# Attention and channel mix on one core: how the first three token groups' q and k are turned, and another order of the opening's steps

## The chip, the cores and the metric

The program runs on one core of one Trainium2 chip. The metric is device time in microseconds, the median of several runs; lower is better. TensorE (PE in the rows, its weight loads PEld), VectorE (DVE), ScalarE (ACT) and SyncE (SP, which only issues transfers here) each work through a queue of their own, in order.

## What is computed

Chunked attention (chunks of 64 tokens, 8 heads of 64) over 8 sequences of 576 tokens, then an RWKV-like channel mix over its 512 outputs.

```python
scores = scale * np.matmul(q_c, k_c.transpose(0, 1, 2, 4, 3))     # within a chunk
attn = softmax(scores);  x = np.matmul(attn, v_c)                  # heads side by side: 512 wide
xk = mu_k * x + (1.0 - mu_k) * x_prev                              # x_prev: the token before
xr = mu_r * x + (1.0 - mu_r) * x_prev
k = np.maximum(xk @ w_k, 0.0)                                      # 512 -> 1024
v = k * k @ w_v                                                    # 1024 -> 512
r = 1.0 / (1.0 + np.exp(-(xr @ w_r)))
return (r * v).astype(np.float32)
```

The weights arrive as 64-bit floats, so their transfers carry 8 bytes for a number, and the kernel makes two float parts (high and low) of each.

## The kernel before

The 4608 tokens are worked in 18 groups of 256 (two tiles of 128). A large product is done as three products of high and low parts (PASSES, line 577). Groups 2 to 17 are written by `group` in the order of the table GROUP. The opening, which covers the loading and conversion of all weights, the attention of tiles 0 to 5 and most of groups 0 and 1, is written in the order of the table START: each word is one step, and each step goes to the end of its engine's queue. No scheduler moves anything after that.

A word is task, number and, after a colon, the engine that does it (A for ScalarE, D for VectorE). The tasks that matter here:

- `nk0`, `nq0`: transfers of group 0's k and q in natural layout, 512 KB each; `v0`: of tile 0's v in four pieces; `swk0` to `swk3`, `swr0`, `swr1`, `swv0` to `swv3`: of pieces of the three weights, 1 MB each. All go through SP's queue.
- `cwk0.0` to `.2` and `hwk0.0`, `.1`: the conversion of such a piece on ScalarE and VectorE.
- `T0.0` to `T0.7`: the turning of group 0's q (0 to 3) and k (4 to 7). Even numbers are eight small products with the identity on TensorE (function `f_tr`, line 357; tiles trq and trk), odd ones copy the result to qT or kT (`f_move`). The partition of a natural tile is a token pair, so a step before takes the even or the odd tokens of the whole group: 128 partitions in, 64 columns of the array, 128 columns streamed, and both column halves of the array at work.
- `S0.0` to `.5`: scores of tile 0 (line 400, 16 products of 64x64 in the four quarters of the array), maximum, subtraction, exponential, sum, division. Scores of a tile need its tokens of qT and kT, which here means all four turning steps of the group.
- `P0.0`, `.1`, `.2`: turning of the probabilities (line 464, pt), copy, product with v (line 484, xps); `Mk`, `Mr`: the token mixes; `K00` to `K03`: the first product of group 0 by quarters of w_k (line 593, pk); `R00`, `R01`: the gate's product by tiles (line 647, pr); `V`: the product with w_v (line 681, pv).
- `W:n`: n products of a 128x128 zero tile with itself (line 1186, warm), whose result nobody reads. They occupy TensorE's queue like any other product. Each shows as two records in the trace, as every plain float product does.

```python
            if name == "W":
                for _ in range(int(e)):
                    nc.tensor.matmul(warm, idle, idle, start=True, stop=True)
            else:
                fn, engine_of = first.pop(name)
                fn(e or engine_of)
```

The rotating PSUM tiles set further waits: ps_k has two buffers for trq, trk and pk together, ps_s has one for scores and turned probabilities.

Of the kernel before, what the change touches and what calls it, by code (L numbers as in the profile page):

```python
# [16 lines left out]
P = 128  # L17
# [7 lines left out]


START = """
mu.0:A nk0.0 nq0.0 swr0.0 W:9 T0.4 T0.6 T0.5:A swr1.0 T0.7:A T0.2 T0.3:D nk1.0 T0.0 mu.1 T0.1:A
cwr0.1:A W:1 S0.0 cwr0.0:A P0.3:D S0.1:D S0.2:D S0.3:A cwr0.2:D v0.0 S0.4:D W:7 S1.0 nq1.0 W:5
T1.6 S1.1:D cwr1.1:A mu.2:A S0.5:D S1.2:D T1.4 P0.0 hwr0.0:A swk3.0 cwr1.0:A T1.7:A S1.3:A  # L30
cwr1.2:D P0.1:A W:3 P0.2 T1.5:A hwr0.1:D S1.4:D P0.4:A hwr1.0:A Mk0.0:D S1.5:D T1.0 T1.2 T1.1:A
Mr0.0:D v1.0 swk0.0 P1.0 Mk0.1:D T1.3:A P1.3:D P1.1:A Mr0.1:A nk2.0 cwk3.0:A W:3 S2.0 Mr0.2:D
S2.1:D nq2.0 W:5 S3.0 P1.2 P1.4:A hwr1.1:D v2.0 S2.2:D R00.0 S2.3:A cwk0.0:A T2.4 cwk3.1:A
S3.1:D Mk1.0:D S2.4:D Mr1.0:D cwk0.1:A S2.5:D T2.5:A T2.6 S3.2:D swk2.0 swk1.0 Mk0.2:A Mr1.1:A
P2.0 T2.7:A T2.2 Mk1.1:D cwk0.2:D T2.0 Mk0.3:D P2.1:A Mk1.2:A S3.3:A Mr1.2:D T2.3:A P2.2
cwk3.2:D hwk0.0:A hwk0.1:D Mk1.3:D T2.1:A S3.4:D P2.3:D hwk3.0:A cwk2.0:A cwk2.1:A S3.5:D
hwk3.1:D P2.4:A v3.0 R01.0 cwk2.2:D cwk1.1:A P3.3:D cwk1.0:A K00.0 K00.1:A P3.0 cwk1.2:D
hwk2.0:A K03.0 P3.1:A S4.0 hwk1.0:A Mk2.0:D hwk2.1:D P3.2 K03.1:A swv1.0 K00.2:A P3.4:A v5.0
Mr2.0:D K03.2:A hwk1.1:D Mr2.1:D S5.0 Mk2.1:D K02.0 R00.1:A Mk3.0:D Mr2.2:D cwv1.0:A swv0.0
Mr3.0:D swv2.0 K00.3:A Mk3.1:D K01.0 K00.4:D R01.1:A cwv1.1:A Mk2.2:A K03.3:D Mr3.1:A Mr3.2:D  # L40
v4.0 K01.1:A Mk3.2:A K03.4:D K01.2:D Mk2.3:D Mk3.3:D cwv2.0:A cwv2.1:A K02.1:A R10.0 cwv2.2:D
cwv0.0:A R11.0 K10.0 S4.1:D cwv1.2:D K02.2:A K11.0 cwv0.1:A hwv2.0:A K01.3:A cwv0.2:D K01.4:D
hwv0.0:A P4.3:D bq3.0 K10.1:A K10.2:A hwv2.1:D K12.0 hwv1.0:A swv3.0 R10.1:A hwv0.1:D S4.2:D
R11.1:A S5.1:D V001.0 S4.3:A hwv1.1:D S5.2:D V001.1 V001.2 V001.3 S4.4:D K02.3:A K10.3:A S4.5:D
S5.3:A K02.4:D cwv3.0:A S5.4:D P4.0 V001.4 cwv3.1:A S5.5:D K12.1:D P4.1:A cwv3.2:D P5.0
hwv3.0:D P5.1:A V001.5 P4.2 hwv3.1:D K12.2:D P5.2 K12.3:A P4.4:A K10.4:D bk3.0 K11.1:D Mk4.0:D
V001.6 K11.2:A V001.7 K11.3:A K13.0 D7.0:D V001.9:D K11.4:D P5.3:D V001.8:D K12.4:D V11.0 V11.1
V10.0 v6.0 Mr4.0:D K13.1:A V10.1 K13.2:A V10.2 P5.4:A K13.3:D V10.3 V11.2 V10.4 Mk4.1:D Mk5.0:D
K13.4:D V10.5 V11.3 V11.4 V11.5 Mk4.2:D V11.6 Mk5.1:D Mr4.1:A Mr4.2:D V10.6 v7.0 D7.1:D V11.7
D6.0:D Mk4.3:D D6.1:D Mk5.2:D Mr5.0:D V11.8:D Mk5.3:D Mr5.1:D V10.7 V10.8:D Mr5.2:D  # L50
"""


# [26 lines left out]
def tile_chunk_attention_channel_mix(  # L80
# [501 lines left out]
    def moe_k(g, fp):  # L582
        def f_mm(_):
            pk = T[f"pk{g}{fp}"] = ps_k.tile([P, 2, G], F32, tag="k", name=f"pk_{g}_{fp}")
            xk = T[f"xk{g}"]
            for e in range(2):
                f = 2 * fp + e
                n = 0
                for cb in range(NB):
                    for a, b in PASSES:  # L590
                        parts = tok if (g > SPLIT and f == n == 0) or (g, f, n) == (1, 0, 0) else (slice(0, G),)
                        for part in parts:
                            nc.tensor.matmul(  # L593
                                pk[:, e, part],
                                wk[a][:, cb, f * P : (f + 1) * P],
                                xk[b][:, cb, part],
                                start=(n == 0 and part is parts[0]),
                                stop=(n == 3 * NB - 1),
                                skip_group_check=True,
                            )  # L600
                        n += 1

        def f_relu(e):
            if g >= SPLIT:
                if fp == 0:
                    T[f"rr{g}"] = mx.tile([P, NF, G], F32, tag="kk", name=f"rr_{g}", bufs=4)
                r = T[f"rr{g}"][:, 2 * fp : 2 * fp + 2, :]
            else:
                r = mo.tile([P, 2, G], F32, tag="relu", name=f"relu_{g}_{fp}")
            T[f"r{g}{fp}"] = r  # L610
            if e == "D":
                nc.vector.tensor_scalar(r, T[f"pk{g}{fp}"], 0.0, None, ALU.max)
            else:
                nc.scalar.activation(r, T[f"pk{g}{fp}"], AF.Relu)  # L614

        def f_sq(e):
            r = T[f"r{g}{fp}"]
            if e == "D":
                nc.vector.tensor_tensor(r, r, r, ALU.mult)
            else:  # L620
                nc.scalar.activation(r, r, AF.Square)  # L621

        def f_hi(e):
            if f"kk{g}" not in T:
# [664 lines left out]
```

## Time and profile before

| | |
|---|---|
| median of 3 runs | 562.23 us (562.0 to 562.52) |
| the profiled execution's own time | 561.84 us |
| its span, first to last instruction | 560.1 us |
| busy share of the span: PE / PEld / DVE / ACT | 99% / 94% / 83% / 62% |
| granted TensorE clock | 1.00 |

The time of the profiled execution is 1.74 us over its span, and 0.39 us under the median of the runs. The busy share of PE includes the fillers `W`, so it doesn't say how much of the span is useful.

### The profile page before, as it was taken

The numbers are of one execution on the slowest core, as the hardware profiler recorded it, in microseconds if no ns is written. First come the engines' busy times: TensorE is split into PE (matmuls) and PEld (weight loads), VectorE is DVE, ScalarE is ACT, GpSimd is POOL, SyncE is SP. The second block draws the span as 40 slices with busy tenths as digits, with TensorE's granted clock in tenths as the row PEclk, the third lists the DMA queues.
The fourth block names the chain that finished last, engine by engine and source line by source line (L and its number), as shares of the span: only waits on it lengthen the run. The fifth ranks groups of instructions, "written<-read, shape, count | busy, mean of one in ns | idle before, by whom it ended". The sixth has DMA issues, their size and how long they took to land.

```text
span 560.1 us, 15245 instructions
## 1 busy us (share of the span) xinstructions
PE 553.5 (99%) x6432; PEld 526.1 (94%) x6432; DVE 462.8 (83%) x789; ACT 346.1 (62%) x509; POOL 0.7 (0%) x6
## 2 busy tenths in 40 slices
PE   9999999999999999999999999999999999999997
PEld 8888999999999999999999999999999999999997
DVE  2999999999897879787888978887888788876834
ACT  5899941739474756657565747483929292938461
POOL 0000000000000000000000000000000000000000
PEclk9999999999999999999999999999999999999999
DMA  9997534444343433421243434343343402010011
GB/s 284 278 285 204 133 76 94 69 69 110 67 107 66 94 69 79 69 72 40 57 67 94 66 89 66 91 71 90 65 99 59 103 1 76 3 45 33 3 38 37
DMA packets 184276, 49.24 MB, mean 88 GB/s; under 512 B 169608, under 2 KB 176272, under 8 KB 184208
## 3 DMA queue, kind: packets, MB, share of 16 engines
q1 hardware_dynamic: 183904, 48.01, 37.9%
q8 instruction: 50, 0.82, 0.7%
q10 hardware_dynamic: 304, 0.27, 0.1%
q14 instruction: 18, 0.15, 0.1%
HBM read 38.80 MB, written 9.44 MB: 86 GB/s over the span
## 4 chain that ended last, share of the span: by engine, by line
PE 90%; ACT 7%; DMA 2%; DVE 0%; issue 0%; ACTq 0%
PE pk L593 33%; PE pr L647 16%; PE vx L870 15%; PE vyz L870 11%; PE pv L681 6%; PE xps L1058 3%; PE s L973 3%; PE pt L1040 2%; DMA k_ring<-in_k 2%; PE warm L1186 1%; ACT wk L141 1%; PE trk L357 1%; ACT wv_st L295 1%; ACT wv_st L299 1%; ACT relu L614 0%; ACT wk_st L299 0%
## 5 line engine op out<-in xcount | busy, mean ns | idle before, releaser
L593 PE MATMUL pk<-xkhi,wk 128*128 128x256 f32 (+1 forms) x1167 | 202.0, 276 | 0.2 <-ACT relu L614 0.2
L593 PEld LDWEIGHTS pk<-xkhi,wk 128*128 128x128 f32 x1167 | 177.1, 188 | 0.7 <-ACT relu L614 0.4
L593 PE MATMUL pk<-xklo,wk 128*128 128x256 f32 x576 | 160.0, 278 | 0.1
L593 PEld LDWEIGHTS pk<-xklo,wk 128*128 128x128 f32 x576 | 108.2, 188 | 0.5 <-DVE xklo L566 0.5
L614 ACT ACTIVATE rr<-pk 128x512 f32<-128x512 f32 x60 | 35.3, 589 | 114.3 <-PE pk L593 114.3
L647 PE MATMUL pr<-wr,xrhi 128*128 128x512 f32 x288 | 90.4, 395 | 0.0
L870 PE MATMUL vx<-b,ks 128*128 128x256 f32 x540 | 68.5, 276 | 0.0
L870 PE MATMUL vyz<-b,kk 128*128 128x256 f32 x540 | 68.5, 276 | 0.0
L870 PEld LDWEIGHTS vyz<-b,kk 128*128 128x128 f32 x540 | 64.5, 188 | 0.0
L870 PEld LDWEIGHTS vx<-b,ks 128*128 128x128 f32 x540 | 64.5, 188 | 0.0
L647 PEld LDWEIGHTS pr<-wr,xrhi 128*128 128x128 f32 x288 | 52.7, 188 | 10.3
L647 PE MATMUL pr<-wr,xrlo 128*128 128x512 f32 x144 | 56.2, 390 | 0.0
L899 ACT ACTIVATE u<-vx 128x256 f32<-128x256 f32 x30 | 11.5, 384 | 54.3 <-PE vx L870 54.3
L708 DVE TENSOR_TENSOR kk<-rr,kk 128x1024 fp32r<-128x1024 f32 x30 | 35.4, 1222 | 10.7 <-ACT kk L854 10.6
L621 ACT ACTIVATE rr<-rr 128x512 f32<-128x512 f32 x60 | 38.0, 633 | 1.9
L708 DVE TENSOR_TENSOR xklo<-mk,xkhi 128x1024 fp32r<-128x1024 f32 x15 | 18.4, 1225 | 25.1 <-ACT xkhi L1130 25.1
L681 PE MATMUL pv<-b,kk 128*128 128x256 f32 (+1 forms) x290 | 34.3, 278 | 0.0
L681 PEld LDWEIGHTS pv<-b,kk 128*128 128x128 f32 x290 | 33.4, 188 | 0.1
L647 PEld LDWEIGHTS pr<-wr,xrlo 128*128 128x128 f32 x144 | 27.0, 188 | 5.7
L708 DVE TENSOR_TENSOR ks<-ss,ks 128x512 fp32r<-128x512 f32 x45 | 28.3, 684 | 0.0
L1120 DVE SCALAR_TENSOR_TENSOR mk<-d,mu,x 128x256 f32<-128x256 f32 (+3 forms) x80 | 27.7, 413 | 0.4
L1120 DVE SCALAR_TENSOR_TENSOR mr<-d,mu,x 128x256 f32<-128x256 f32 (+3 forms) x80 | 27.5, 411 | 0.0
(119 smaller groups left out, 839.4 us busy)
## 6 DMA issues: line engine op xcount, KB each, us to landing
v<-in_v SPq DMA_DIRECT2D x144, 64.0 KB, 2.6
out<-sg SPq DMA_DIRECT2D x34, 256.0 KB, 2.3
q_ring<-in_q SPq DMA_DIRECT2D x192, 36.0 KB, 2.1
k_ring<-in_k SPq DMA_DIRECT2D x192, 36.0 KB, 2.2
wk_st<-in_moe_w_k SPq DMA_DIRECT2D x4, 1024.0 KB, 9.4
wv_st<-in_moe_w_v SPq DMA_DIRECT2D x4, 1024.0 KB, 7.5
wr_st<-in_moe_w_r SPq DMA_DIRECT2D x2, 1024.0 KB, 8.1
k_ring<-in_k SPq DMA_DIRECT2D x2, 512.0 KB, 7.3
```

What stands on the lines that cost most here:

```text
L593: nc.tensor.matmul(pk[:, e, part], wk[a][:, cb, f * P : (f + 1) * P], xk[b][:, cb, part], start=(n == 0 and part is parts[0]), stop=(n == ...
L614: nc.scalar.activation(r, T[f"pk{g}{fp}"], AF.Relu)
L621: nc.scalar.activation(r, r, AF.Square)
L647: nc.tensor.matmul(pr, xr[a][:, cb, tl * TT : (tl + 1) * TT], wr[b][:, cb, :], start=(n == 0), stop=(n == 3 * NB - 1),)
L681: nc.tensor.matmul(T[f"pv{g}{tl}"][:, cols[c]][:, part], kk[a][:, f, tok[tl]], quarter(f // HF, c)[:, b, f % HF, part], start=(f == 0 and ...
L708: nc.vector.tensor_tensor(to, x, y, ALU.subtract)
L870: nc.tensor.matmul(to, a[i][:, f, :], weight(w, j, f), start=first and f == 0 and n == 0, stop=f == HF - 1 and n == 2, skip_group_check=True,)
L899: nc.scalar.activation(T[f"u{g}"][n // 2][:, n % 2], src(), AF.Copy)
L973: nc.tensor.matmul(T[f"s{g}"][halves[e], j, tl, hp, :], qT[halves[j], hp, cols], kT[halves[j], hp, cols], start=True, stop=True,)
L1040: nc.tensor.transpose(out=T[f"pt{g}"][:, tl, hp, :], in_=T[f"pg{g}"][:, tl, 2 * hp : 2 * hp + 2, :], identity=ident,)
L1058: nc.tensor.matmul(T[f"xps{g}"][halves[c], 2 * j + a, tl * TT + e * CH : tl * TT + (e + 1) * CH], T[f"v{2 * g + tl}"][halves[j], hp, e, :] ...
L1120: nc.vector.scalar_tensor_tensor(out=to[:, cb, s : s + w], in0=T[f"d{g}"][:, cb, s : s + w], scalar=mu[:, cb : cb + 1], in1=T[f"xg{g}"][:, ...
```

## The change

Three things change. First, a turning step takes one tile of 128 tokens (64 token pairs, so 64 partitions) instead of every second token of the group: 16 products of 64x64 instead of 8 with 128 partitions and 128 streamed columns. Its number says which tile: `T0.0` and `T0.4` are tile 0, `T0.2` and `T0.6` tile 1. Scores of a tile then need two turning steps, not four. Second, START is another order: the two key pieces wk0 and wk1 are loaded and converted ahead of those of w_r, K00 and K01 stand ahead of R00 and R01, and the fillers stand elsewhere and number 54 instead of 33. Some copies change between ScalarE and VectorE (23 steps; ScalarE has 5 more and VectorE 5 fewer than before). Third, which first product is issued in two halves: K12's and K11's instead of K10's in group 1 (f is 2 and 4), and of the V products the first of `V001` alone.

```diff
 START = """
-mu.0:A nk0.0 nq0.0 swr0.0 W:9 T0.4 T0.6 T0.5:A swr1.0 T0.7:A T0.2 T0.3:D nk1.0 T0.0 mu.1 T0.1:A
+mu.0:A nk0.0 W:9 T0.6 T0.4 P0.3:D nq0.0 T0.7:D swk0.0 swk1.0 T0.5:A W:3 T0.0 T0.2 T0.1:A W:1
+S0.0 T0.3:A cwk0.0:A S1.0 S0.1:D v0.0 S0.2:D S1.1:D S1.2:D cwk0.1:A S0.3:A S0.4:D cwk0.2:D
...
         for nm, to in (("q", qT), ("k", kT)):
-            for r in range(2):
+            for tl in range(2):
...
                     for hp in range(HP):
-                        for j in range(2):
-                            nc.tensor.matmul(
-                                x[halves[j], hp, :],
-                                T[f"{nm}{g}"][:, j * HP + hp, r, :],
-                                ident,
-                                start=True,
-                                stop=True,
-                            )
-
-                def f_move(e, nm=nm, to=to, r=r):
-                    copy(e, to.rearrange("p h (c r) -> p h r c", r=2)[:, :, r, :], T[f"tr{nm}{r}{g}"])
+                        for r in range(2):
+                            for j in range(2):
+                                nc.tensor.matmul(
+                                    x[halves[j], hp, r, :],
+                                    T[f"{nm}{g}"][halves[tl], j * HP + hp, r, :],
+                                    ident[halves[tl], halves[tl]],
+                                    start=True,
+                                    stop=True,
+                                )
+
+                def f_move(e, nm=nm, to=to, tl=tl):
+                    to = to.rearrange("p h (t c r) -> p h t r c", t=2, r=2)
+                    copy(e, to[:, :, tl], T[f"tr{nm}{tl}{g}"])
...
-                        parts = tok if (g > SPLIT and f == n == 0) or (g, f, n) == (1, 0, 0) else (slice(0, G),)
+                        parts = tok if (g > SPLIT and f == n == 0) or (g == 1 and f in (2, 4) and n == 0) else (slice(0, G),)
...
-                            parts = tok if first and (g, tl) in ((0, 0), (1, 1)) else (slice(0, HD),)
+                            parts = tok if first and g == 0 else (slice(0, HD),)
```

TensorE's queue from the program's first product, before (trk is the turned k, trq the turned q, s scores, pt turned probabilities, xps their product with v):

```order
L1186 MATMUL warm<-idle 128x128 x9
L357 MATMUL trk_0_141<-ident,k_ring 64x128 x8
L357 MATMUL trk_0_150<-ident,k_ring 64x128 x8
L357 MATMUL trq_0_163<-ident,q_ring 64x128 x8
L357 MATMUL trq_0_174<-ident,q_ring 64x128 x8
L241 MATMUL mu_t<-ident,mus 128x8
L1186 MATMUL warm<-idle 128x128
L400 MATMUL s_188<-kT,qT 64x64 x16
L1186 MATMUL warm<-idle 128x128 x7
L400 MATMUL s_188<-kT,qT 64x64 x16
L1186 MATMUL warm<-idle 128x128 x5
L357 MATMUL trk_1_252<-ident,k_ring 64x128 x8
```

The same place after the change (lines are 4 or 5 further on):

```order
L1191 MATMUL warm<-idle 128x128 x9
L361 MATMUL trk_0_138<-ident,k_ring 64x64 x16
L361 MATMUL trk_0_155<-ident,k_ring 64x64 x16
L1191 MATMUL warm<-idle 128x128 x3
L361 MATMUL trq_0_184<-ident,q_ring 64x64 x16
L361 MATMUL trq_0_201<-ident,q_ring 64x64 x16
L1191 MATMUL warm<-idle 128x128
L405 MATMUL s_220<-kT,qT 64x64 x32
L1191 MATMUL warm<-idle 128x128 x25
L469 MATMUL pt_299<-ident,p_262 128x128 x4
L242 MATMUL mu_t<-ident,mus 128x8
L1191 MATMUL warm<-idle 128x128 x2
```

Both tiles' scores now stand together, a run of 25 fillers follows them, and group 1's turning, which stood between the scores and the first pt, has moved behind it.

TensorE's queue further on, before, from group 1's turned k to the first gate product (pr, the start of R00):

```order
L357 MATMUL trk_1_266<-ident,k_ring 64x128 x8
L464 MATMUL pt_275<-ident,p_210 128x128 x4
L1186 MATMUL warm<-idle 128x128 x3
L484 MATMUL xps_292<-pT_287,v_214 64x64 x16
L357 MATMUL trq_1_320<-ident,q_ring 64x128 x8
L357 MATMUL trq_1_329<-ident,q_ring 64x128 x8
L464 MATMUL pt_275<-ident,p_210 128x128 x4
L1186 MATMUL warm<-idle 128x128 x3
L400 MATMUL s_372<-kT,qT 64x64 x16
L1186 MATMUL warm<-idle 128x128 x5
L400 MATMUL s_372<-kT,qT 64x64 x16
L484 MATMUL xps_292<-pT_287,v_344 64x64 x16
```

After the change, from the second pt to the first key product (pk, the start of K00):

```order
L469 MATMUL pt_299<-ident,p_262 128x128 x4
L361 MATMUL trk_1_397<-ident,k_ring 64x64 x16
L489 MATMUL xps_323<-pT_314,v_316 64x64 x16
L1191 MATMUL warm<-idle 128x128 x2
L361 MATMUL trq_1_437<-ident,q_ring 64x64 x16
L1191 MATMUL warm<-idle 128x128 x4
L361 MATMUL trq_1_466<-ident,q_ring 64x64 x16
L405 MATMUL s_486<-kT,qT 64x64 x16
L1191 MATMUL warm<-idle 128x128
L361 MATMUL trk_2_512<-ident,k_ring 64x64 x16
L405 MATMUL s_486<-kT,qT 64x64 x16
L361 MATMUL trk_2_552<-ident,k_ring 64x64 x16
```

What stands ahead of the first large product is no longer R00 after two turnings but K00 after two turnings and half of group 2's. Between the rows shown, after the change, lie the first xps, a turned k and a run of 7 fillers.

SP's queue from its first transfer to group 2's k, before:

```order
L184 DMA k_ring<-in_k 128x8x128
L184 DMA q_ring<-in_q 128x8x128
L291 DMA wr_st<-in_moe_w_r 128x2x1024 x2
L184 DMA k_ring<-in_k 128x8x128
L199 DMA v_214<-in_v 64x4x64 x4
L184 DMA q_ring<-in_q 128x8x128
L291 DMA wk_st<-in_moe_w_k 128x4x512
L199 DMA v_344<-in_v 64x4x64 x4
L291 DMA wk_st<-in_moe_w_k 128x4x512
L184 DMA k_ring<-in_k 32x8x128
L184 DMA k_ring<-in_k 96x8x128
```

And after the change:

```order
L185 DMA k_ring<-in_k 128x8x128
L185 DMA q_ring<-in_q 128x8x128
L292 DMA wk_st<-in_moe_w_k 128x4x512 x2
L200 DMA v_257<-in_v 64x4x64 x4
L185 DMA k_ring<-in_k 128x8x128
L292 DMA wr_st<-in_moe_w_r 128x2x1024
L200 DMA v_316<-in_v 64x4x64 x4
L185 DMA q_ring<-in_q 128x8x128
L185 DMA k_ring<-in_k 32x8x128
L185 DMA k_ring<-in_k 96x8x128
L292 DMA wr_st<-in_moe_w_r 128x2x1024
```

Ahead of group 2's k stand three weight pieces of 1 MB where there were four; ahead of group 1's q stand three where there were two.

## Rows read from the trace of the kernel before

**Rows 1.** Busy time by stage: us, then PE, PEld, DVE, ACT, POOL.

```profile
5.26:28.95 23.69, 22.14 (x390) 19.27 (x390) 18.66 (x41) 18.28 (x26) 0.00 (x0) 1.00 1.12 303
...
62.28:560.10 497.82, 494.50 (x5644) 473.14 (x5644) 412.59 (x690) 293.68 (x436) 0.00 (x0) 1.00 0.32 69
```

**Rows 2.** Timeline of PE, 0 to 31 us: start, us, what, records, idle before.

```profile
1.05 4.21 PE L1186 MATMUL warm<-idle 128*128 128x128 f32 x18 [1.05 <-DVE idle L130]
...
9.34 0.49 PE L1186 MATMUL warm<-idle 128*128 128x128 f32 x2
9.98 0.69 PE L400 MATMUL s<-kT,qT 64*64 64x64 f32 x32 [0.15 <-ACT qT L141]
10.61 1.83 PE L1186 MATMUL warm<-idle 128*128 128x128 f32 x14
12.37 0.69 PE L400 MATMUL s<-kT,qT 64*64 64x64 f32 x32
12.99 1.38 PE L1186 MATMUL warm<-idle 128*128 128x128 f32 x10
14.30 1.97 PE L357 MATMUL trk<-ident,k_ring 128*64 128x128 f32 x32
16.23 0.63 PE L464 MATMUL pt<-ident,p 128*128 128x128 f32 x4
16.70 0.83 PE L1186 MATMUL warm<-idle 128*128 128x128 f32 x6
17.62 0.69 PE L484 MATMUL xps<-pT,v 64*64 64x64 f32 x32
18.24 1.97 PE L357 MATMUL trq<-ident,q_ring 128*64 128x128 f32 x32
20.71 0.66 PE L464 MATMUL pt<-ident,p 128*128 128x128 f32 x4 [0.49 <-DVE p L434]
21.20 0.83 PE L1186 MATMUL warm<-idle 128*128 128x128 f32 x6
22.05 0.69 PE L400 MATMUL s<-kT,qT 64*64 64x64 f32 x32
22.67 1.38 PE L1186 MATMUL warm<-idle 128*128 128x128 f32 x10
24.08 0.69 PE L400 MATMUL s<-kT,qT 64*64 64x64 f32 x32
...
25.17 0.73 PE L647 MATMUL pr<-wr,xrhi 128*128 128x512 f32 x2
...
28.95 1.97 PE L357 MATMUL trk<-ident,k_ring 128*64 128x128 f32 x32 [0.77 <-DMA k_ring<-in_k]
```

**Rows 3.** The same timeline of PE, 40 to 63 us: first rows of steps.

```profile
40.47 0.37 PE L593 MATMUL pk<-xkhi,wk 128*128 128x256 f32 x1
...
43.72 0.69 PE L400 MATMUL s<-kT,qT 64*64 64x64 f32 x32 [0.27 <-ACT pT L141]
...
45.27 0.38 PE L593 MATMUL pk<-xkhi,wk 128*128 128x256 f32 x1
...
50.84 0.63 PE L647 MATMUL pr<-wr,xrhi 128*128 128x512 f32 x2
...
56.30 0.33 PE L593 MATMUL pk<-xkhi,wk 128*128 128x128 f32 x2
...
62.28 0.38 PE L593 MATMUL pk<-xkhi,wk 128*128 128x256 f32 x1 [0.24 <-ACT relu L614]
```

**Rows 4.** Timeline of PE, 91 to 94 us: a whole group's scores.

```profile
92.25 1.16 PE L973 MATMUL s<-kT,qT 64*64 64x64 f32 x64
```

**Rows 5.** Timeline of DVE, 0 to 80 us: the second tile's low part of xk, group 0.

```profile
36.62 0.69 DVE L566 TENSOR_TENSOR xklo<-mixk,xkhi 128x512 fp32r<-128x512 f32 x1
```

**Rows 6.** Instructions on the tile trk: duration ns min/median/max, starts, forms.

```profile
L357 PEld LDWEIGHTS trk<-ident,k_ring x96: 132/137/232, 5.2 to 30.5; 128*64 128x64 f32 x96
```

**Rows 7.** Sum of five stretches of 10 us from 10 to 60 us.

```profile
sum 50.00, PE 48.19 PEld 43.10 DVE 47.45 ACT 46.94 POOL 0.00; mean PE 9.64 PEld 8.62 DVE 9.49 ACT 9.39 POOL 0.00
```

More of the change, by code (lines that the diff above doesn't have):

```diff
@@ L27 @@
 START = """
-mu.0:A nk0.0 nq0.0 swr0.0 W:9 T0.4 T0.6 T0.5:A swr1.0 T0.7:A T0.2 T0.3:D nk1.0 T0.0 mu.1 T0.1:A
[L29 to L50, printed above, removed]
+mu.0:A nk0.0 W:9 T0.6 T0.4 P0.3:D nq0.0 T0.7:D swk0.0 swk1.0 T0.5:A W:3 T0.0 T0.2 T0.1:A W:1
@@ new lines @@
+S0.0 T0.3:A cwk0.0:A S1.0 S0.1:D v0.0 S0.2:D S1.1:D S1.2:D cwk0.1:A S0.3:A S0.4:D cwk0.2:D
+S0.5:D W:25 P0.0 nk1.0 mu.1 cwk1.0:A cwk1.1:A cwk1.2:D S1.3:A hwk0.0:A swr1.0 P0.1:A v1.0 W:2
+P0.2 nq1.0 P0.4:A nk2.0 mu.2:A S1.4:D P1.3:A hwk0.1:D swr0.0 T1.6 Mk0.0:D cwr1.1:A S1.5:D
+hwk1.0:A Mr0.0:D W:7 P1.0 P1.1:A Mk0.1:D T1.4 Mr0.1:A hwk1.1:D T1.7:A P1.2 W:2 T1.0 P1.4:A
+Mk0.2:A Mk1.0:D T1.5:A T1.1:A W:4 T1.2 cwr1.0:A Mr0.2:D T1.3:A S2.0 Mk1.1:D S2.1:D Mk0.3:D W:1
+T2.4 Mk1.2:A S3.0 T2.5:A v2.0 T2.6 Mk1.3:D S2.2:D K00.0 cwr1.2:D T2.7:A nq2.0 S2.3:A S3.1:D
@@ new lines @@
+swk3.0 S2.4:D cwr0.0:A cwr0.1:A S3.2:D K00.1:A cwr0.2:D S2.5:D hwr1.0:A S3.3:A hwr0.0:A K01.0
+hwr1.1:D swk2.0 hwr0.1:D Mr1.0:D K01.1:A S3.4:D P2.0 P2.1:A T2.0 T2.2 P2.2 K01.2:A T2.1:A
+T2.3:A cwk3.1:A Mr1.1:A S3.5:D R00.0 cwk3.0:A Mr1.2:D P3.0 cwk2.0:A R01.0 P2.3:D cwk2.1:A
+cwk3.2:D hwk3.0:A K00.2:A P3.1:D v3.0 cwk2.2:D swv1.0 hwk3.1:D P2.4:A P3.3:D S4.0 hwk2.0:A
+R01.1:A S5.0 P3.2 swv2.0 Mk2.0:D P3.4:A v5.0 hwk2.1:D Mr2.0:D K03.0 Mk2.1:D swv0.0 K00.3:A
+Mr2.1:A bk3.0 Mk3.0:D R00.1:A K01.3:A K02.0 Mr2.2:D cwv2.1:A Mk3.1:D Mk2.2:D K00.4:D Mk3.2:A
@@ new lines @@
+Mk2.3:D Mk3.3:D K03.1:A K01.4:D v4.0 R10.0 K03.2:D cwv0.0:A K02.1:A K03.3:A Mr3.0:D R10.1:A
+Mr3.1:D K03.4:D cwv2.0:A cwv1.1:A S4.1:D cwv1.0:A Mr3.2:D K02.2:A K11.0 cwv0.1:A K10.0 cwv2.2:D
+hwv2.0:D hwv2.1:D cwv0.2:D K02.3:A K02.4:D R11.0 S5.1:D S4.2:D K11.1:A R11.1:A K10.1:A hwv0.0:A
+K12.0 S4.3:A cwv1.2:D hwv0.1:D swv3.0 K13.0 V001.0 hwv1.0:A S4.4:D hwv1.1:D S4.5:D S5.2:D
+V001.1 D6.1:D cwv3.0:A bq3.0 V001.2 cwv3.1:A V001.3 K10.2:A K10.3:A K11.2:A cwv3.2:D S5.3:A
+S5.4:D hwv3.0:A K11.3:A hwv3.1:D S5.5:D V001.4 P4.0 K11.4:D K12.1:A V001.5 P5.0 P4.3:D V001.6
@@ L51 @@
+P4.1:D K10.4:D D7.0:D P5.1:A K13.1:D V001.7 V001.8:D P4.2 K12.2:A K12.3:A P5.2 v6.0 V10.0
+P4.4:A P5.3:A V001.9:D V10.1 V10.2 K12.4:D Mk4.0:D K13.2:A Mk4.1:D V11.0 V10.3 V10.4 V11.1
+D6.0:D K13.3:A P5.4:D K13.4:D Mk4.2:A Mk5.0:D Mr4.0:D Mk4.3:D Mk5.1:D V10.5 D7.1:D V10.6
+Mk5.2:A Mr5.0:D V11.2 V10.7 Mr4.1:A V11.3 Mr4.2:D V11.4 v7.0 V11.5 V11.6 Mk5.3:D V10.8:D V11.7
+V11.8:D Mr5.1:A Mr5.2:D
 """
@@ L350, in move_qk, with f_tr @@
         for nm, to in (("q", qT), ("k", kT)):
-            for r in range(2):
-                def f_tr(_, nm=nm, r=r):
-                    x = T[f"tr{nm}{r}{g}"] = ps_k.tile([P, HP, P], F32, tag="k", name=f"tr{nm}{r}_{g}")
-                    for hp in range(HP):
-                        for j in range(2):
-                            nc.tensor.matmul(
-                                x[halves[j], hp, :],
-                                T[f"{nm}{g}"][:, j * HP + hp, r, :],
-                                ident,
-                                start=True,
-                                stop=True,
-                            )
-                def f_move(e, nm=nm, to=to, r=r):
-                    copy(e, to.rearrange("p h (c r) -> p h r c", r=2)[:, :, r, :], T[f"tr{nm}{r}{g}"])
+            for tl in range(2):
+                def f_tr(_, nm=nm, tl=tl):
+                    x = T[f"tr{nm}{tl}{g}"] = ps_k.tile(
+                        [P, HP, 2, CH], F32, tag="k", name=f"tr{nm}{tl}_{g}"
+                    )
+                    for hp in range(HP):
+                        for r in range(2):
[6 more added lines that the diff above has]
+                                    stop=True,
+                                )
+                def f_move(e, nm=nm, to=to, tl=tl):
+                    to = to.rearrange("p h (t c r) -> p h t r c", t=2, r=2)
+                    copy(e, to[:, :, tl], T[f"tr{nm}{tl}{g}"])
                 do(f_tr, "P")
```

## Prediction

> **What bounds the kernel now.** I read the busy time by stage first. From 62 us to the end TensorE is busy for 494.5 of 497.8 us, on work that the change doesn't touch, while VectorE and ScalarE have a sixth and two fifths of that stretch free [rows 1]. Whatever time TensorE loses or saves before 62 us therefore comes out at the end, unchanged; nothing later can take it up. So the question is one of a ledger: how much of TensorE's time in the opening is not useful work, now and after.
>
> I read that off the timeline of TensorE, from the start of one group of instructions to the start of the next, since the ends overlap. The first run of fillers (9 of them, from 1.05 us for 4.21 us) waits for the first k and is the same in both orders, so it cancels. The other 24 stand in six runs [rows 2]: 9.34 to 9.98, 0.64; 10.61 to 12.37, 1.76; 12.99 to 14.30, 1.31; 16.70 to 17.62, 0.92; 21.20 to 22.05, 0.85; 22.67 to 24.08, 1.41. Sum 6.89 us. What a filler costs comes from the runs of 7 and of 5 (14 and 10 records): (1.76 - 1.31) / 2 = 0.225 us each and 0.185 us for a run as such. A run of 3 then is 0.86, measured 0.92 and 0.85.
>
> Then the waits that no filler covers. The two turnings from 18.24 to the pt at 20.71 take 2.47, the two from 14.30 to 16.23 take 1.93: 0.54 lost, to a probability that VectorE was late with [rows 2]. The gate product R00 from 25.17 to 28.95 takes 3.78 [rows 2], where two such take 5.46 from 50.84 to 56.30: 1.05 lost, to group 2's k, which lands late [rows 2, 3]. K03 takes 3.25 (40.47 to 43.72) where two take 5.57 (45.27 to 50.84): 0.46. The two from 56.30 to 62.28 take 5.98: 0.41 [rows 3]. Sum 2.46 us. Not useful after the first run: 6.89 + 2.46 = 9.35 us.
>
> **The fillers after.** START now holds 54, so 45 behind the first nine, in runs of 3, 1, 25, 2, 7, 2, 4 and 1. At the prices above: 45 x 0.225 + 8 x 0.185 = 11.6 us. They run whether anything waits or not. Against 6.89 that is +4.7. The lowest bound drops the price of the runs as such: 10.1, +3.2.
>
> **The bare waits after.** At most all 2.46 us of now can go. The one for group 2's k should: in SP's queue three 1 MB pieces stand ahead of it in place of four, and TensorE asks for it later. The others come from VectorE and ScalarE, which are busy for 95% and 94% of 10 to 60 us [rows 7]; the same work is due, but TensorE comes later to each step (next paragraph), so there is more cover. The new place that I looked at is K00. It needs the low part of the second tile's xk. By adding prices along the new order, TensorE gets to the first pt at about 17.4 us: 5.26, four turning steps 4.0, runs of 3, 1 and 25 for 0.86 + 0.41 + 5.81, two score steps 1.1. Before, the first pt starts at 16.23, with two more turning steps (1.93 us) done [rows 2]. To K00 there are 13.7 us more: six turnings 6.0, the runs of 2, 7, 2, 4 and 1 for 4.5, two pt and two xps 2.1 (0.47 and 0.62 now [rows 2]), two score steps 1.1. So K00 is reached at about 31.1 us. Before, VectorE wrote that low part at 36.62 to 37.3 [rows 5]. But of VectorE's words up to it START had 34 before and has 23 now: w_r's conversion and most of tiles 2 and 3's softmax are behind it. Eleven steps of at least 0.6 us (a short one shows 0.69 with its end) are 6.6 us, which puts it at 30.7 or sooner. Just in time, so I take 0.2 us of bare waits in all, with 0 and 2.5 (as many as now) as bounds: -2.3, from -2.5 to 0.
>
> **The turning steps.** There are 12. Now two take 1.93 us together [rows 2], 0.965 each, for 8 rounds of two column halves and two records. A new step has 16 products of 64x64, 32 records, and all of one step lie in one half of the array's rows. The trace has no such step; the nearest is the scores, the same 64x64 products in all four quarters. A group's scores, 64 records, take 1.16 us, a tile's, 32 records, 0.69 [rows 2, 4]: 8 more rounds of four cost 0.47, so a round is 0.059 us. A new step can use two quarters at a time, so it is 16 rounds: 0.94 us. Upper bound: with the end that a tile's scores show from start to start (9.98 to 10.61 is 0.63 [rows 2], less 0.47) 1.10. As turnings now stand next to steps of the same shape in part, I take 1.00: 12 x 0.035 = +0.4, bounds -0.3 and +1.6. Three of the score steps now stand beside turnings of their own shape and can lose some 0.1 us of end each: -0.3. Together +0.1.
>
> The rows speak on one more point. While a turning's product runs, the next one's weights are loaded: the load lasts 137 ns at the median [rows 6], yet two steps of 16 rounds take 1.93 us, 121 ns for a round, though every load and every product there uses all rows of the array [rows 2, 6]. The Trainium skill (TensorE: Matmul & The Clock Gate, Part 3, The mechanism) says that a load overlaps with running products only when it is for another row group. In this kernel's turning steps the trace does not agree: all rows are one group there, and the round is shorter than the load. By that rule each of the 16 rounds of a new step would bear its load, and with the page's figure of columns / 1.2 ns for one (53 ns for 64) the 12 steps would cost 10 us more, an estimate from the page; by the rows nothing.
>
> **The rest.** The first product in halves: three places before (K10, V001, V11) and three after (K11, K12, V001), each the same columns in two pieces: 0. The copies that change engine (five more on ScalarE) are hidden as long as TensorE is the later one; uncovered, they would be part of the bare waits. The weight pieces' order in SP's queue costs nothing by itself: ahead of group 1's q there is one piece of 1 MB more, but TensorE asks for it at 24.6, by the sum above, instead of 18.24 us [rows 2].
>
> **Sum.** +4.7 - 2.3 + 0.1 = +2.5 us on the profiled execution's 561.84, so 564.3; the median of the runs lies 0.39 above that execution, so 564.8.
>
> **Rivals.**
> - *Uncovered waits stay.* ScalarE and VectorE have hardly any room, and the new order asks for xk six microseconds earlier. If K00, or the pt that stand behind a softmax, wait as much in sum as now (2.5 us) or more, fillers come on top of waits: +4.7 + 0.4, so 567.3 and above. Against it: 11 fewer VectorE steps ahead of K00.
> - *The opening breaks even.* All fillers at the lower bound (+3.2), all bare waits gone (-2.46), turnings at 0.94 and shorter score ends (-0.6): +0.1, about 562.4. It needs every bound at once in one direction, or some of the useful work, which I count as fixed, to run closer together.
> - *The quarters run side by side (faster).* If a new turning step went at the pace of a tile's scores, 0.63 us instead of 0.965 [rows 2], that is 12 x 0.335 = -4.0 where I put +0.4. Then -1.9, so 560.4. It decides from a step of about 0.79 us downwards (12 x 0.21 is the 2.5 us). Against it: the 16 products of a step all use one row half and stand in one piece in the queue; the next row half comes with the next step. The same page of the Trainium skill states that products start and end in program order, which no row here contradicts.
> - *Loads are exposed.* If a load of the length shown (132 ns at the least [rows 6]) were borne by each round, 12 x 16 x 0.132 = 25 us, 590. The trace speaks against it, as said where the page's rule stands.
>
> **Chances.** Forecast 0.61; waits stay 0.14; breaks even 0.16; side by side 0.08; loads exposed 0.01. A change of 0.2%, 1.1 us, is about what a measurement of this kernel can tell from none. The forecast, the waits and the loads are slower: 0.61 + 0.14 + 0.01, of which some 0.02 of the forecast's lower tail falls within 0.2%: 0.74. Breaks even, that tail and 0.01 of the side by side case: 0.19. The rest of it is faster: 0.07. The range leaves out the faster case and the far end of the waits: from 562.5 (break even) to 567.3.
>
> **What the profile after would show.** Warm products: 108 records, of which 90 behind the first run, in eight runs of which the one of 25 lasts about 5.8 us. A pair of turnings side by side (T0.6 and T0.4) 1.9 to 2.1 us. First pt at 17 to 17.7 us, first pk at 31 to 32 us. Few idle entries above 0.2 us on TensorE before 70 us. The first whole group's scores, at 92.25 us now [rows 4], near 94.8, and from there on the same distances as before. I am wrong if a turning step takes under 0.8 us, if those scores start before 93.3 us, or if the part behind them changes its length.

## The result and the profile after

The changed kernel takes 567.99 us (median of five executions, 567.63 to 571.29) where the kernel before took 562.25 (562.0 to 562.66) beside it: ratio 1.0109, interval 1.0095 to 1.0123, so 5.7 us slower. The forecast of 564.8 had the direction; the loss is more than twice the 2.5 us of its sum and lies just above its range. The execution that was profiled is the longest of the five: 571.29 us, span 569.5, granted clock 0.994; the others have spans of 565.8 to 566.5 at a clock of 1.0, and that difference is explained below.

The timeline of TensorE after, as in [rows 2]: start, us, what, records, idle before.

```profile
1.05 4.21 PE L1191 MATMUL warm<-idle 128*128 128x128 f32 x18 [1.05 <-DVE x L506]
5.19 2.25 PE L361 MATMUL trk<-ident,k_ring 64*64 64x64 f32 x64
7.37 0.94 PE L1191 MATMUL warm<-idle 128*128 128x128 f32 x6
8.23 1.91 PE L361 MATMUL trq<-ident,q_ring 64*64 64x64 f32 x64
10.07 0.49 PE L1191 MATMUL warm<-idle 128*128 128x128 f32 x2
10.49 1.16 PE L405 MATMUL s<-kT,qT 64*64 64x64 f32 x64
11.58 0.71 PE L1191 MATMUL warm<-idle 128*128 128x128 f32 x4
13.06 5.29 PE L1191 MATMUL warm<-idle 128*128 128x128 f32 x46 [0.77 <-issue]
18.20 0.60 PE L469 MATMUL pt<-ident,p 128*128 128x128 f32 x4
...
23.47 0.66 PE L469 MATMUL pt<-ident,p 128*128 128x128 f32 x4 [0.56 <-DVE p L439]
...
33.92 1.76 PE L361 MATMUL trk<-ident,k_ring 64*64 64x64 f32 x27 [1.82 <-issue]
35.60 0.58 PE L598 MATMUL pk<-xkhi,wk 128*128 128x256 f32 x1
...
43.25 0.60 PE L469 MATMUL pt<-ident,p 128*128 128x128 f32 x4
```

Two idle entries name no engine but "issue": 0.77 us inside the run of 25 fillers and 1.82 us in the middle of a turning step (T2.6). The products of the kernel before have none in the whole trace. The windows of 5 us around the second one (PE, PEld, DVE, ACT, POOL busy, granted clock, share of the DMA engines, GB/s) show what follows it:

```profile
25.00:30.00 5.00, 5.00 (x149) 4.56 (x145) 3.91 (x9) 4.43 (x8) 0.00 (x0) 1.00 1.16 249
30.00:35.00 5.00, 3.18 (x93) 2.92 (x93) 4.32 (x6) 1.44 (x3) 0.00 (x0) 0.83 1.09 294
35.00:40.00 5.00, 5.00 (x33) 4.88 (x30) 2.65 (x5) 3.23 (x4) 0.00 (x0) 0.50 1.14 305
40.00:45.00 5.00, 5.00 (x81) 4.83 (x81) 3.08 (x4) 4.28 (x7) 0.00 (x0) 0.99 0.92 339
```

TensorE stood still in most of 32.1 to 33.9, and the granted clock is 0.50 (1.2 of 2.4 GHz) until 40. K00 and K01 take 43.25 - 35.60 = 7.65 us there, where 48 such products take 5.57 to 5.76 at the full clock. With the slow half of T2.6 the fall costs about 2.8 us. That is most of the 3.0 to 3.7 us by which this execution's span exceeds those of the other four, whose clock reads 1.0. No trace of those four is kept, so how long their own stalls were is not known.

Further on, the scores that stood as one piece in [rows 4] come as two halves:

```profile
95.43 0.69 PE L978 MATMUL s<-kT,qT 64*64 64x64 f32 x32
...
101.25 0.69 PE L978 MATMUL s<-kT,qT 64*64 64x64 f32 x32
101.88 0.38 PE L598 MATMUL pk<-xkhi,wk 128*128 128x256 f32 x1
```

Group 2's 96 first products run from 101.88 to 113.57, 11.69 us; before, from 93.34 to 104.33, 10.99. From there to the end it is 455.9 us, against 455.8: the part behind has kept its length.

### The profile page after: what moved, and what is told of

The parts are those of the page before. It is cut to its first block, busy times and chain, and to the rows that moved or that the text cites. A ratio compares the mean times of both kernels' runs of the same rounds, so it can differ in the third digit from the quotient of the medians.

```text
span 569.5 us, 15711 instructions
## 1 busy us (share of the span) xinstructions
PE 561.8 (99%) x6666; PEld 535.1 (94%) x6666; DVE 462.4 (81%) x786; ACT 348.8 (61%) x512; POOL 0.7 (0%) x6
## 4 chain that ended last, share of the span: by engine, by line
PE 98%; DVE 1%; issue 0%; ACT 0%
PE pk L598 35%; PE pr L652 17%; PE vx L875 15%; PE vyz L875 11%; PE pv L686 6%; PE xps L1063 3%; PE s L978 3%; PE warm L1191 2%; PE pt L1045 2%; PE trk L361 1%; PE trq L361 1%; PE xps L489 1%; PE s L405 1%; PE pt L469 0%; DVE wk L314 0%
## 5 line engine op out<-in xcount | busy, mean ns | idle before, releaser
L598 PE MATMUL pk<-xkhi,wk 128*128 128x256 f32 (+1 forms) x1168 | 204.2, 278 | 0.0
L598 PEld LDWEIGHTS pk<-xkhi,wk 128*128 128x128 f32 x1168 | 178.9, 190 | 0.5
```

The lines of the kernel that those rows point to most:

```text
L598: nc.tensor.matmul(pk[:, e, part], wk[a][:, cb, f * P : (f + 1) * P], xk[b][:, cb, part], start=(n == 0 and part is parts[0]), stop=(n == ...
```

## The experiments

All times are medians beside runs of the kernel before on the same chip (561.9 to 562.6). "Old turning" is the one by token parity, "new turning" the one by tiles; a filler is a `W` product. Both halves of the first experiment keep the split first products of the change, so what that split does alone was not measured.

**1. The two halves of the change, and the fillers of the new order.**

The new order (START and the split first products) with the old turning; a few words had to move, since a tile's scores then need all four steps:

```diff
-S0.0 T0.3:A cwk0.0:A S1.0
+T0.3:A S0.0 cwk0.0:A S1.0
```

> The new order and its 54 fillers with the old turning (by token parity); the copy T0.3 stands ahead of S0.0, as the old turning needs. Theory S (supply): part of the loss is TensorE running out of instructions (0.77 us in the run of 25 fillers, 1.82 us in the middle of T2.6, both put down to issue), because the new turning doubles the records of 12 steps while the DMA engines are full. With 192 fewer products and their loads the two stalls go or shrink: 565 to 566 us. Theory F (order and fillers): all of the loss is in the order; only the turning's own 0.4 us goes: about 567.5 us.

567.47 us (566.81 to 569.47), ratio 1.0093 (1.0077 to 1.0108). The order alone is 4.9 us slower, nearly the whole change, as theory F had it, without one entry that names the issue. Its TensorE timeline:

```profile
10.76 1.16 PE L401 MATMUL s<-kT,qT 64*64 64x64 f32 x64 [0.30 <-ACT qT L142]
11.85 5.85 PE L1187 MATMUL warm<-idle 128*128 128x128 f32 x50
17.61 0.63 PE L465 MATMUL pt<-ident,p 128*128 128x128 f32 x4
...
22.91 0.66 PE L465 MATMUL pt<-ident,p 128*128 128x128 f32 x4 [0.48 <-DVE p L435]
...
29.78 0.69 PE L401 MATMUL s<-kT,qT 64*64 64x64 f32 x32 [0.78 <-ACT qT L142]
...
33.49 0.39 PE L594 MATMUL pk<-xkhi,wk 128*128 128x256 f32 x1
```

The step of VectorE that ends the first softmax (it divides p), first here, then in the kernel before:

```profile
16.78 0.68 DVE L435 TENSOR_TENSOR p<-p,z 128x512 f32<-128x512 f32 x1
```

```profile
14.80 0.68 DVE L434 TENSOR_TENSOR p<-p,z 128x512 f32<-128x512 f32 x1
```

Here it ends at 17.46, 2.0 us later than before, and the first pt follows 0.15 us behind it. VectorE first takes the maximum at 11.99 (10.75 before), behind both tiles' scores, and now works two steps of the second tile's softmax ahead of that division where one stood before.

The new turning in the old order (the edit as against the changed kernel):

```diff
 START = """
-mu.0:A nk0.0 W:9 T0.6 T0.4 P0.3:D nq0.0 ...
+mu.0:A nk0.0 nq0.0 swr0.0 W:9 T0.4 T0.6 T0.5:A ...
```

> The old order and its 33 fillers with the new turning by tiles. Theory S: the doubled records alone bring stalls for instructions of 1 to 2 us: 563.3 to 564.5 us. Theory F: the turning costs its 0.4 us and frees the scores of a tile somewhat earlier: 562.2 to 562.7 us.

568.34 us (567.78 to 568.5), ratio 1.0103 (1.0089 to 1.0116). The turning alone is as slow as both together, far above what either theory gave. Of what TensorE waited for in its first 110 us, what names the issue (total, times, longest):

```profile
PE s L404 <- issue: 2.6, 3, 1.4
PE trq L360 <- issue: 2.2, 1, 2.2
```

These are 4.8 us, and the granted clock was 0.50 for 3.4 us from 22.8 us on.

The changed kernel without its 45 later fillers (`W:3`, `W:1`, `W:25`, `W:2`, `W:7`, `W:2`, `W:4`, `W:1` left out):

> The changed kernel without the 45 fillers behind the first nine. If the fillers are pure extra work, as the forecast's ledger had it, most of their 11.7 us goes, less what then shows as waits: 560 to 563 us. If they stand where TensorE would wait anyway (the run of 25 ahead of the first softmax, the run of 7 ahead of the second), the time hardly moves or gets worse through a lower granted clock: 566 to 571 us. Theory S adds that 180 fewer records bring less stall: up to 2 us off either.

571.32 us (570.12 to 572.96), ratio 1.0159 (1.0142 to 1.0177), slower than with them. The first pt comes at 16.26 us, 1.9 earlier than with the fillers, but after a wait, and the clock falls:

```profile
16.26 1.09 PE L469 MATMUL pt<-ident,p 128*128 128x128 f32 x4 [5.68 <-DVE p L439]
```

```profile
10.00:15.00 5.00, 0.57 (x32) 0.44 (x32) 4.22 (x8) 3.71 (x5) 0.00 (x0) 0.72 1.13 278
15.00:20.00 5.00, 3.26 (x57) 2.87 (x59) 3.35 (x8) 3.65 (x7) 0.00 (x0) 0.50 1.10 314
```

So most of the run of 25 stands in a wait for VectorE's first softmax. The order itself has made that hole: the softmax ends later, and group 1's turning, which lay there before, needs a k that SP issues at 7.3 us where it was 3.8.

The changed kernel with each four fillers as one product of 512 columns (its first run ends 0.4 us later, since the zero tile is larger):

```diff
-                for _ in range(int(e)):
-                    nc.tensor.matmul(warm, idle, idle, start=True, stop=True)
+                for n in [4] * (int(e) // 4) + [1] * (int(e) % 4):
+                    nc.tensor.matmul(warm[:, : n * P], idle[:, :P], idle[:, : n * P], start=True, stop=True)
```

> The changed kernel with every four fillers in one product of 512 columns: the same filler time in 24 products instead of 54, so 60 records and 60 loads fewer ahead of the stall. Theory S: the stall in the run of 25 goes and the one in T2.6 comes later or shrinks: 566 to 567 us. Theory F: 568 us as before.

567.28 us (566.75 to 568.11), ratio 1.0087 (1.0074 to 1.01). With fewer instructions for the same filling there is no entry that names the issue, clock 1.0. The stalls go, which theory S expected, but the time hardly does: it still loses 4.7 us, the order's part.

**2. Is it the number of instructions?** The kernel before, with nothing changed but each turning product cut into two column halves:

```diff
-                        for j in range(2):
-                            nc.tensor.matmul(
-                                x[halves[j], hp, :], T[...][:, j * HP + hp, r, :], ident, ...
+                        for c in range(2):
+                            for j in range(2):
+                                nc.tensor.matmul(
+                                    x[halves[j], hp, halves[c]], T[...][:, j * HP + hp, r, :], ident[:, halves[c]], ...
```

> The kernel before, with each turning product (128 rows of the array, 128 columns) cut into two products of 64 columns: 16 products for a step where there were 8, 32 records for 16, the same columns in all, the order and the copies as before. Theory (TensorE's instructions come too slowly by the DMA queue that fetches them while the loads keep the DMA engines full): idle entries of 0.4 us and more that name the issue, not another engine, show on TensorE in the first 50 us, 2.5 us or more in sum, as with the new turning in the old order, and the time is 566 to 568.5. Rival (products of 64 by 64 in one row half are what costs): those idle entries do not show, and the time is 562.2 to 563.2.

569.1 us (566.99 to 570.65), ratio 1.0116 (1.0096 to 1.0135): 6.8 us lost without a turning of 64 by 64, a new order or an added filler, and slightly more than the theory gave. The timeline shows them in the middle of pieces that wait for nobody:

```profile
22.46 2.46 PE L358 MATMUL trq<-ident,q_ring 128*64 128x64 f32 x59 [2.68 <-issue]
...
31.35 0.40 PE L401 MATMUL s<-kT,qT 64*64 64x64 f32 x13 [1.77 <-issue]
...
52.81 0.33 PE L401 MATMUL s<-kT,qT 64*64 64x64 f32 x3 [1.19 <-issue]
```

The second stall hits a score step that wasn't touched. The geometry of the new turning is not the cause; the number of instructions is.

The places of the stalls say the same. Count TensorE's records, products and loads together, from the start of each trace. The 15 idle entries on TensorE's products that name the issue, in all traces kept, stand 176 to 189 records past a multiple of 256, whatever step they hit. The next experiment shows what comes in pieces of that size.

**3. Do the loads matter, or the pace alone?** TensorE's instructions come by a DMA queue of their own (q8 on the page: 52 packets after, 50 before, of 16 KB; its records, 13332 and 12864, make 52.1 and 50.3 times 256). In the changed kernel the queues' rows of 30 to 35 us (packets, MB, share of 16 engines' time in that window) hold one such packet,

```profile
q1 hardware_dynamic: 1133, 1.46, 107.8%
q8 instruction: 1, 0.02, 1.7%
```

which lasts from 31.24 to 32.58, and TensorE goes on at 33.92. To tell pace from loads I added 96 products to the kernel before, in a place with the DMA engines nearly free and in one where they are full. The first two pairs never reached the pace that they were meant to have:

```diff
+                    nc.tensor.matmul(y, ident, ident[:, :64], start=True, stop=True)
```

> The kernel before with 96 added products of 64 columns in one piece (192 records, the identity times itself, read by nothing), where the loads leave the DMA engines nearly free: behind the second xps of tile 5, near 75.5 us. At the 29.6 ns for a record of the split turnings they take 5.7 us by themselves, so 568.0 without a stall. Theory that full DMA engines hold up the fetching of instructions: no idle entry that names the issue within the piece or right behind it, 567.6 to 568.3. Rival that the pace alone is the cause (so many small instructions use up what is fetched ahead, however free the DMA engines are): 1 to 2 us of such an entry here too, 569 to 570.5.

> The same 96 added products early, behind K03 near 43.7 us, where the DMA engines are busy all the time by the windows of the kernel before. Both theories expect a stall of 1 to 2 us that names the issue here; by the DMA theory it is missing in the late place, by the pace alone it is as long there. Without any stall 567.5 to 568.0 (two waits of 0.4 us behind the place may be covered by the piece), with one 569 to 570.5. If neither place shows one, a single dense piece is not enough and the supply has to be short over several steps.

583.78 and 583.07 us: both pieces take 21.6 us, 113 ns a record, without an entry that names the issue. I took the common place that all write for the reason and spread them over eight places:

> As the late piece of 96 added products (behind the second xps of tile 5, DMA engines nearly free), but product after product into eight different places of its PSUM tile, as the turnings write, not all into one (which took 113 ns a record). At 29.6 ns a record 5.7 us, so 568.0 without a stall. Theory that full DMA engines hold up the fetching of instructions: no idle entry that names the issue in the piece or right behind it, 567.6 to 568.4. Rival that the pace alone is the cause: an entry of 1 to 2 us here too, 569 to 570.5.

> The same 96 products into eight places, early, behind K03 near 43.7 us, where the DMA engines are busy all the time. Both theories expect an entry of 1 to 2 us that names the issue, 568.5 to 570; by the DMA theory the late place has none, by the pace alone it is as long there. If neither place has one, 567.3 to 568, and one dense piece of 192 records is not enough.

583.8 and 582.46 us, the same. So the place written isn't it. What these pieces share is the full load of 128 by 128 with every product:

```profile
L1190 PEld LDWEIGHTS burst<-ident x192: 186/192/192, 76.0 to 97.3; 128*128 128x128 f32 x192
```

The third pair runs as the turnings do, with weights of 64 columns for the two column halves in turn:

```diff
+                    j = halves[i % 2]
+                    nc.tensor.matmul(y[j, i // 2 % 8], ident[:, j], ident[:, :64], start=True, stop=True)
```

> The 96 added products once more, now as the split turnings run them: the weights are 64 columns wide and go to the one and the other half of the array's columns in turn, eight places each (with full loads of 128 by 128 a record took 112 ns, whatever place it wrote). Late, near 75.5 us, DMA engines nearly free. At 29.6 ns a record 5.7 us: 567.7 to 568.2 without a stall. Theory that full DMA engines hold up the fetching of instructions: no idle entry that names the issue. Rival that the pace alone is the cause: one of 1 to 2 us here too, 568.9 to 570.3.

> The same piece early, behind K03 near 43.7 us, where the DMA engines are busy all the time. Both theories expect an entry of 1 to 2 us that names the issue, 568.3 to 569.8; by the DMA theory the late place has none, by the pace alone it is as long there. If neither has one, 567.2 to 567.9, and one dense piece of 192 records is not enough.

Late: 568.03 us (567.5 to 568.62), ratio 1.0098 (1.0079 to 1.0118), 5.8 us for the piece, in one row:

```profile
76.07 5.82 PE L1191 MATMUL burst<-ident 128*64 128x64 f32 x192
```

Early: 569.65 us (569.4 to 570.2), ratio 1.0129 (1.0114 to 1.0144), in two:

```profile
43.24 4.82 PE L1191 MATMUL burst<-ident 128*64 128x64 f32 x157
49.62 1.26 PE L1191 MATMUL burst<-ident 128*64 128x64 f32 x35 [1.56 <-issue]
...
53.08 0.33 PE L400 MATMUL s<-kT,qT 64*64 64x64 f32 x3 [0.65 <-issue]
```

The windows of the two places, late first (DMA share and GB/s are the last two):

```profile
76.00:78.00 2.00, 2.00 (x78) 1.93 (x69) 1.97 (x5) 1.63 (x4) 0.00 (x0) 1.00 0.05 9
78.00:80.00 2.00, 2.00 (x76) 2.00 (x74) 0.74 (x2) 0.81 (x2) 0.00 (x0) 1.00 0.00 0
```

```profile
44.00:46.00 2.00, 2.00 (x76) 2.00 (x74) 2.00 (x6) 1.64 (x3) 0.00 (x0) 1.00 1.01 399
46.00:48.00 2.00, 2.00 (x71) 1.98 (x66) 2.00 (x6) 0.00 (x0) 0.00 (x0) 1.00 0.83 324
48.00:50.00 2.00, 0.44 (x15) 0.38 (x14) 0.06 (x1) 0.00 (x0) 0.00 (x0) 1.00 0.08 27
```

The same products at the same pace: stalls of 1.56 and 0.65 us where the piece begins with the DMA engines full, none where they are free. The stalls themselves fall behind the full stretch (share 0.08 in the last row). The instruction packet ahead of the first starts at 46.91 us, 371 records late by the count at the end of this document; in the late place the two packets start 200 and 204 late. The full engines without the pace (the slow pieces) and the pace without the full engines both bring no stall; it takes both.

**4. Does a filler cost its length?**

The old turning in the new order (as in the first experiment) without the first two later runs:

```diff
-T0.5:A W:3 T0.0 T0.2 T0.1:A W:1
+T0.5:A T0.0 T0.2 T0.1:A
```

> The old turning in the new order, without the first two runs of fillers behind the first nine (of 3 and of 1). Theory (the ledger: these two fill nothing, all that they take comes out at the end): 1.28 us less than with them by their distances (0.86 + 0.42), so 566.2, if no wait takes their place. Rival (the steps behind them wait for VectorE and ScalarE in any case): 567.2 to 567.7, with the wait ahead of the first pt or of the third group of tokens' scores longer by as much.

566.66 us (565.79 to 567.98), ratio 1.0073 (1.0057 to 1.0088): 0.8 less, not 1.28. The interval is too wide to tell these two apart; the trace shows why the gain is smaller: the wait for qT ahead of the first scores grew from 0.30 to 0.72 us.

Then also `W:25` to `W:18`:

> The old turning in the new order without the first two later runs of fillers, and with the run of 25 cut to 18. Theory of the ledger (fillers in excess of the wait): 7 x 0.225 = 1.6 us less than with 25, so 565.1. Rival (the run stands in the wait for the first softmax, so the pt behind it waits instead): 566.3 to 566.9, with a wait of 1 us or more for VectorE's p ahead of the first pt.

566.47 us (566.35 to 566.76), ratio 1.008 (1.0067 to 1.0092): seven fillers, 1.6 us, bring next to nothing. In their place stands:

```profile
16.83 0.63 PE L465 MATMUL pt<-ident,p 128*128 128x128 f32 x4 [1.47 <-DVE p L435]
```

And the kernel before with `W:7` to `W:4` and `W:5` to `W:2`:

> The kernel before with the run of 7 fillers cut to 4 and the run of 5 cut to 2. Theory of the ledger (fillers run whether anything waits or not, and what they take comes out at the end): 6 x 0.225 = 1.35 us less, 561.0. Rival (they stand in waits for the probabilities of VectorE): the pt behind them waits for as much, 562.0 to 562.6.

562.75 us (562.13 to 563.28), ratio 1.0009 (1.0 to 1.0017): nothing gained. New waits in the list of TensorE's waits take 0.8 + 0.5 = 1.3 us, the 1.35 that the six fillers took, and an entry that names the issue has come to it:

```profile
PE pt L464 <- DVE p L420: 0.8, 1, 0.8
...
PE s L400 <- DVE p L420: 0.5, 1, 0.5
...
PE s L400 <- issue: 0.3, 1, 0.3
```

**5. Two more runs.** The changed kernel once more:

> The changed kernel once more, for the trace of an execution without the fall of the clock. Theory: span 565.8 to 566.6, clock 1.0; the idle entries that name the issue stand there too, shorter than the 1.82 us of the first profile, under 1.8 us in sum; and the part behind 105 us has the same distances as in the kernel before. Rival (the stall is part of every execution and only the clock differs): entries of 2.4 us or more in sum with the clock at 1.0.

575.64 us, span 573.9: neither. A stall of 2.10 us stands at the same place (38.26, in T2.6), with the clock at 0.54 behind it, and TensorE worked at half pace for much longer at the start: the first pair of turnings takes 3.25 us instead of 2.18, and the fillers and scores up to 16 us are as slow. The views print a granted clock of 1.00 there, but the trace has no row of the clock before 17.34 us, where the other runs' first row, of 1.00, begins at 4.6 to 7.0. One execution says no more than that both can vary.

The kernel before with group 2's k ahead of a weight piece in SP's queue, and that piece's conversions moved back:

```diff
-Mr0.0:D v1.0 swk0.0 P1.0 ... nk2.0 cwk3.0:A
+Mr0.0:D v1.0 nk2.0 P1.0 ... swk0.0 cwk3.0:A
```

> The kernel before, with group 2's k ahead of the first weight piece of the k that stands before it in SP's queue, and the two conversions of that piece moved back behind the other k pieces' on ScalarE. Theory (the 1.05 us ahead of group 2's first turning is a wait for that load alone): the wait goes and the time falls by 0.6 to 1.05 us, 561.2 to 561.7. Rival (VectorE, ScalarE or the weight piece that now lands later ends the next wait): the same length comes back at the first pk, 562.0 to 562.8.

563.45 us (562.97 to 565.38), ratio 1.0021 (1.0011 to 1.0031): a little slower, and above both ranges. R00 now takes 2.95 us instead of 3.78, so that wait was for the load indeed; but the turned q behind it waits for a copy on ScalarE,

```profile
34.26 1.09 PE L357 MATMUL trq<-ident,q_ring 128*64 128x128 f32 x16 [1.34 <-ACT kT L141]
```

and more comes back than went. No version beat the kernel before.

## Why the prediction was wrong in size

**Right.** *The direction.* *That TensorE's opening decides:* the part from group 2's first products to the end has 10.99 + 455.8 us before and 11.69 + 455.9 after. *The price of a filler:* the eight runs last 13.1 us from start to start, 11.8 without the 0.77 and 0.56 that stand as waits in or behind them; the forecast was 11.6. *The turning step:* the two pairs of group 0 take 2.18 + 1.84 = 4.02 us, against 3.93 before, +0.02 a step where I put +0.035. *Group 2's k* is no longer waited for, and K00 did not wait for xk.

Of the signs, the first pt (18.20, by the stall ahead of it) and the first pk (35.60) came later than put down, the run of 25 took 5.85 us without its stall, as put down, and the first whole group's scores, near 94.8, came in halves at 95.43 and 101.25.

Neither rival on the array's quarters came true: steps that no stall hit stood at 0.87 to 1.09 us, not below 0.8, and no load was exposed. By the rule of the Trainium skill that the prediction weighed (TensorE: Matmul & The Clock Gate, Part 3, The mechanism), which lets a load overlap only for another row group, they should have grown by some 0.8 us each (the 10 us of that estimate over 12 steps); this trace does not agree. The same section of the Trainium skill also lets a load for the background weight buffer go ahead; these rows can't tell whether that is what happens. The added pieces show what the pace goes with instead, all on all 128 rows: 30 ns a record with weights of 64 columns in the two column halves in turn, 112 with weights of 128. Whether it is the turn or the narrower load was not told apart.

The prediction also took from the Trainium skill (the same page and section) that products start in program order, and had no row against it. The changed kernel's trace does not agree: two records of xps start at 24.93 and 24.94 us, ahead of the last two of the turned k, at 24.98 and 24.99, which stands in front of xps in the queue.

**Wrong: the step "bare waits after", -2.3 us.** It took 0.2 us of waits for the new order, "so there is more cover". The order alone, free of supply stalls, has from one start to the next 0.30 (qT ahead of the first scores), 0.48 (p) and 0.85 us (qT ahead of tile 2's scores) up to K00, 1.6 in all. From the first pt to K00 I put 13.7 us; it takes 33.49 - 17.61 = 15.88, of which 1.3 are the last two waits and the rest ends of pieces that I left out, with 0.16 for mu_t. To this come 0.7 us in group 2's first products (0.28 of it a second product that waits for the low part of xk; the rest is a pace of 118 in place of 114 ns, whose cause stays open) and 0.4 us for the halved scores (0.15 for a second end; the rest is the same slower pace in the V products beside them): the first half stands 44 of the V products earlier than the second. I had looked for moved instructions in the opening alone, where START sets the order; behind it, the halves of these scores are placed otherwise once the opening is another (with the new turning in the old order they are one piece again, 98.42 us). Together 2.7 us, against 0.2; with the forecast's other terms that gives 567.3, and the order alone measured 567.47. The rival *uncovered waits stay* (0.14) thus had the nearest time, though its condition, 2.5 us of waits or more, came true only in part: 1.6 us are waits ahead of K00.

Behind the wrong step is a wrong reading. I counted fillers as lost time of TensorE that adds to whatever waits. Two cuts of fillers (experiment 4) show that those ahead of the first pt mostly stand in a wait for the first softmax: take them away, and the wait appears. So the first pt's place, 17.4 us, came out nearly right (17.61 in the order alone) for a wrong reason. It is set by VectorE: the softmax ends 0.15 us ahead of it. Its first pt comes 1.38 us later than in the kernel before (16.23) and with 1.93 us less of turning done, so 3.3 of the 4.9 us are lost by then: a softmax that ends 2.0 us later, and less useful work in the wait for it. No run put that work back.

**Missing: the supply of instructions.** No term and no rival of mine had it. I asked what 16 products of 64 by 64 cost on the array, found nothing, and never asked what twice the instructions cost to fetch while the weights load. The new turning alone costs 5.8 us, with 4.8 us of such entries and a stretch at half the clock behind them; the same number of instructions with the old geometry costs 6.8. In the changed kernel's traces the entries are 2.6 and 2.1 us.

**Why the two don't add.** Order alone 4.9, turning alone 5.8, both 5.7. In the changed kernel long runs of fillers use few instructions per microsecond, and a stall that falls into such a run (the 0.77 us) partly replaces a wait for the softmax. Wide fillers remove the stalls and bring only 0.7 us (1.2 by the ratios), with a first run that ends 0.4 later. That this overlap is the whole reason is argued from those rows, not shown by a run of its own.

## What to carry to other kernels

Where loads fill the DMA engines, count a step's instructions as well as its columns: here a piece of 96 small products, at 30 ns a record, ran dry after 157 of its 192 records, and the idle entry then names the issue and no engine. Before a filler is priced, ask what would stand in its place; if a softmax on another engine ends that stretch, only useful work moved into it gains anything. And when an order is rewritten, write down for each such wait which useful work covers it before and after.

## What the runs showed of the hardware

- A packet of 16 KB on the instruction queue lasts 0.9 to 1.9 us, in full and in quiet stretches alike; what differs is when it starts. A packet comes for every 256 of TensorE's records (products and loads counted together). Take the records that have started when a packet starts, less 256 for each packet before it: in the kernel before, that is 265 to 353 for the first five packets, in the full stretch up to 48 us, and 141 to 159 for the next five, up to 100 us. For the packet ahead of the 2.68 us stall with split turnings it is 440. That is worked out from the records' starts; that the loads hold these packets back is argued from it. A late start alone is no stall: with wide fillers it reached 415 without one. After a stall TensorE resumes 1.3 to 1.7 us behind the end of such a packet.
- Around the 1.82 us without a product the granted clock fell to 0.50 for 6.8 us, at the 2.10 us of the repeat for 6.8 too, and at the stalls of 2.16 and 2.68 us for 3.4. In the fillers' absence, with TensorE busy for 0.57 of 5 us, it fell too and was at 0.50 until 39.6 us.
- The first nine fillers run at 213 ns a record, later ones mostly at 112 to 123. In the changed kernel the products of K00 and K01 start 213 ns apart while the granted clock is 0.50, and 113 at 1.00, so the first fillers run at the pace of half the clock. The views print 1.00 there for want of a row: the clock's first row begins only at 4.6 to 7.0 us. The first pair of turnings follows it: 2.02 us where that row begins at 5.48, 2.70 where it begins at 7.03, 3.25 where at 17.34.
